# Replacing a six-step gelu with one ScalarE activation, and a sigmoid silu with a tanh form

## The chip, the cores and the metric

The kernel runs on one core of one Trainium2 chip. The metric is the device time of one execution in microseconds (us); where several runs are quoted, it is their median. The profile is one execution taken by the hardware profiler, a little shorter than the device time of the same run (283.6 against 286.2 us before).

Names used below: PE is TensorE (matmul), PEld its weight loads, DVE is VectorE, ACT is ScalarE, POOL is GpSimd, SP issues most DMAs.

## The reference, cut to what matters

Everything is bf16, with S = 2048 rows and D = 512 columns. One branch is local attention (32 heads, 8 shifted keys), the other a two-stage network with gelu; the second gates the first through a silu.

```python
def reference(x, wqkv, wo, w1, w2, w3, w4):
    xn = layernorm(x)
    s  = local_attention(xn @ wqkv) @ wo              # 8 shifted keys per position, softmax
    h  = gelu_tanh(layernorm(xn) @ w1)                # 4 chunks x 4 column blocks = 16 gelus of 128x512
    x1 = xn + shift_columns(h) @ w2
    h2 = gelu_tanh(layernorm(x1) @ w3) @ w4           # F = 1376: 4 chunks x 11 blocks = 44 gelus
    return x + s * silu(x1 + h2)
```

`gelu_tanh` is `jax.nn.gelu(approximate=True)`.

## The kernel before

The 2048 rows are four chunks of 512. A first stage runs, software-pipelined over the chunks: norms (VectorE), transposes, q/k/v and w1 matmuls, attention logits by products on VectorE (`pw`) reduced by TensorE, softmax, w2. Then comes a handover: the third norm needs statistics of all chunks, and its result goes to DRAM and comes back transposed (`x1n_dram`, `x1nT`). After it come a first w3 block, and a main loop that interleaves attention output, `wo`, the next chunk's w3 and w4.

The gelu took three ScalarE and three VectorE instructions (a sigmoid form of the tanh approximation):

```python
    def gelu_from_psum(pt, dst, nparts):
        # ... three scratch tiles sq, xb, t from a pool
        nc.scalar.activation(sq[:nparts], pt[:nparts], AF.Square, scale=SQK)
        nc.scalar.activation(xb[:nparts], pt[:nparts], AF.Copy)
        nc.vector.tensor_scalar(out=sq[:nparts], in0=sq[:nparts], scalar1=1.0, scalar2=None, op0=ALU.add)
        nc.vector.tensor_tensor(out=t[:nparts], in0=sq[:nparts], in1=xb[:nparts], op=ALU.mult)
        nc.scalar.activation(sq[:nparts], t[:nparts], AF.Sigmoid, scale=GELU_C)
        nc.vector.tensor_tensor(out=dst, in0=xb[:nparts], in1=sq[:nparts], op=ALU.mult)
```

Other parts that the argument touches:

```python
            # stage2(c): attention logits, 8 per chunk
            nc.vector.tensor_tensor(out=pw, in0=qT, in1=kT[:, :, koff : koff + CH], op=ALU.mult)
            # ... 16 small matmuls of pw with a head selector, into lg

    # handover: third norm of all 16 row tiles at once, then chunk by chunk
    def stage3b():
        nc.scalar.activation(rstd3, mv3[:, :, 1], AF.Sqrt, bias=eps_t[:], scale=1.0)
        # ... reciprocal, -mean*rstd
    def stage3c(c):
        # ... xn3 = x1 * rstd3 + nmr3
        nc.sync.dma_start(out=x1n_dram[...], in_=xn3)
        nc.sync.dma_start_transpose(out=x1nT, in_=x1n_dram[...])

    def emit_x2(i):                    # attention output of row tile i
        # ... et_ps: transposed softmax; att_sb: its copy
        for w in range(W):             # 8 products on VectorE
            nc.vector.tensor_tensor(out=prod[:, w, :], in0=vs[:, w, :], in1=att_sb[...], op=ALU.mult)
        # ... o_ps: TensorE sums the 8 with an identity matmul; o_sb, ot_ps, oTt

    def emit_final(i, gch, jj):
        # ... pt_s = oTt @ wo
        nc.vector.tensor_tensor(out=sg, in0=pt_s, in1=gch[:, jj, :], op=ALU.mult)
        # ... ot = x + sg, to DRAM

    def emit_w4(c, h3T, gch):
        # ... pt_t = x1 + h3 @ w4
        nc.scalar.activation(sig, pt_t, AF.Sigmoid)
        nc.vector.tensor_tensor(out=gch[:, jj, :], in0=pt_t, in1=sig, op=ALU.mult)
```

The softmax here doesn't subtract the row's maximum and nothing guards it: scores larger than these inputs give would overflow.

## Time and profile before

| | before |
|---|---|
| time, median of 3 runs | 285.42 us (284.32 to 286.18) |
| span of the profiled run | 283.6 us |
| busy PE / DVE / ACT | 236.5 / 230.4 / 180.6 us |
| 60 gelus: ScalarE steps | 597, 601, 635 ns each |
| 60 gelus: VectorE steps | 291, 422, 422 ns each |

From the page of the kernel before: busy time with its share of the span and the number of instructions, then busy tenths in 40 equal slices (each slice is 7.1 us), and the TensorE clock that was granted, in tenths.

```profile
PE 236.5 (83%) x1652; PEld 109.7 (39%) x1680; DVE 230.4 (81%) x586; ACT 180.6 (64%) x318; POOL 7.2 (3%) x26
...
PE   0349978998699999936978899999998999898991
...
DVE  4998998969948986999989958774598992899544
ACT  1105796797569689750469957995178862788620
...
PEclk9999996999999999995899999999999999999997
```

Two engines are above 80% and no slice has TensorE and VectorE idle together, so no single busy share names the limit. The two dips of PE and PEclk in the middle (slices 18 to 20) are the handover.

The chain of work that ended last, shared out by engine, before:

```profile
PE 41%; DVE 30%; ACT 13%; issue 7%; DMA 5%; SPq 2%; ACTq 0%; DVEq 0%
```

So 43% of the chain runs through VectorE and ScalarE.

The same kernel cut into its stages. Columns: window and its length, then busy us of PE, PEld, DVE, ACT, POOL with counts, granted clock, DMA share, GB/s. The rows are: up to the end of the last w1 block; handover; first w3 block; first to last w4 matmul; tail.

```profile
20.00:109.50 89.50, 82.17 (x735) 39.64 (x748) 76.76 (x155) 67.52 (x112) 5.05 (x14) 0.96 0.14 41
109.50:141.00 31.50, 23.64 (x236) 10.29 (x234) 30.96 (x80) 16.18 (x26) 0.00 (x0) 0.84 0.69 189
141.00:158.50 17.50, 13.20 (x75) 5.68 (x74) 15.46 (x51) 14.57 (x27) 0.00 (x0) 1.00 0.85 256
158.50:274.10 115.60, 110.05 (x577) 49.20 (x587) 86.86 (x240) 79.30 (x149) 0.00 (x0) 1.00 0.43 124
274.10:283.60 9.50, 3.65 (x17) 1.46 (x15) 4.51 (x9) 0.60 (x1) 0.00 (x0) 0.82 0.21 69
```

Read each row by itself. In the handover VectorE is full (30.96 of 31.5 us). In the first w3 block VectorE and ScalarE are both near full (15.46 and 14.57 of 17.5) while TensorE needs 13.2. In the long main loop TensorE is at 95%.

What TensorE waited for in the first w3 block of before (total us, times, longest):

```profile
PE w_ps L445 <- ACT g_xb L164: 2.6, 3, 1.3
PE o_ps L411 <- DVE prod L403: 1.4, 1, 1.4
```

Both engines hold it: `g_xb` is a gelu step on ScalarE, `prod` an attention product on VectorE.

The six gelu steps of before, as groups (busy us, mean ns of one, idle time before them and what ended it):

```profile
L167 ACT ACTIVATE g_sq<-g_t 128x512 bf16<-128x512 bf16 (+1 forms) x60 | 37.1, 635 | 3.7 <-DVE g_t L166 3.2
L164 ACT ACTIVATE g_xb<-w_ps 128x512 bf16<-128x512 f32 (+1 forms) x60 | 36.1, 601 | 0.0
L163 ACT ACTIVATE g_sq<-w_ps 128x512 bf16<-128x512 f32 (+1 forms) x60 | 35.8, 597 | 8.0 <-PE w_ps L445 4.4 <-DVE g_t L166 1.4 <-PE w_ps L258 1.0
L166 DVE TENSOR_TENSOR g_t<-g_sq,g_xb 128x512 bf16<-128x512 bf16 (+1 forms) x60 | 25.3, 422 | 4.0 <-ACT g_xb L164 3.9
L168 DVE TENSOR_TENSOR h3T<-g_xb,g_sq 128x512 bf16<-128x512 bf16 (+1 forms) x44 | 18.5, 422 | 2.7 <-ACT g_sq L167 2.1
L165 DVE TENSOR_SCALAR g_sq<-g_sq 128x512 bf16<-128x512 bf16 (+1 forms) x60 | 17.4, 291 | 8.4 <-ACT g_sq L163 7.4
```

(The sixth step writes `h3T` in 44 cases and `hTp` in the 16 of the first stage.)

### The profile page before, as it was taken

To read this page: it belongs to the slowest core of one execution; us is meant where nothing else is said; L and a number is where in the kernel's file an instruction comes from. 1 tells how busy PE (TensorE), PEld (TensorE's weight loads), DVE (VectorE), ACT (ScalarE), POOL (GpSimd) and SP (SyncE) were. 2 spreads that over 40 slices of the span, in tenths; PEclk is the share of its full clock that TensorE was granted. 3 is DMA by queue.
4 is the path that set the end of the run, shared out by engine and by line. 5 is a ranking of instruction groups with operands and counts; after the bars stand their busy time and mean duration, and the time that the engine had idled before them with its cause. 6 is when DMAs were issued, how large, how long until landed. Compare 5 with 4: busy or idle time off the path is not lost.

```text
span 283.6 us, 4696 instructions
## 1 busy us (share of the span) xinstructions
PE 236.5 (83%) x1652; PEld 109.7 (39%) x1680; DVE 230.4 (81%) x586; ACT 180.6 (64%) x318; POOL 7.2 (3%) x26
## 2 busy tenths in 40 slices
PE   0349978998699999936978899999998999898991
PEld 0234444445344444412433344443444444443440
DVE  4998998969948986999989958774598992899544
ACT  1105796797569689750469957995178862788620
POOL 3000100010020001000000000000000000000000
PEclk9999996999999999995899999999999999999997
DMA  7996020020002005853989888514066664111102
GB/s 222 386 376 156 2 74 2 0 77 0 2 0 77 2 0 178 241 157 116 232 238 275 233 247 265 178 38 113 0 177 195 183 192 147 38 37 37 39 0 92
DMA packets 40311, 35.65 MB, mean 126 GB/s; under 512 B 11250, under 2 KB 38752, under 8 KB 40288
## 3 DMA queue, kind: packets, MB, share of 16 engines
q1 hardware_dynamic: 39680, 33.24, 39.5%
q0 software_dynamic: 608, 2.11, 2.2%
q8 instruction: 13, 0.21, 0.3%
q14 instruction: 10, 0.08, 0.1%
HBM read 26.94 MB, written 6.31 MB: 117 GB/s over the span
## 4 chain that ended last, share of the span: by engine, by line
PE 41%; DVE 30%; ACT 13%; issue 7%; DMA 5%; SPq 2%; ACTq 0%; DVEq 0%
PE w_ps L458 12%; PE qk_ps L229 10%; DVE prod L403 6%; DVE pw L269 5%; PE v_ps L246 5%; PE o_ps L411 4%; PE w_ps L445 4%; ACT g_sq L163 4%; DVE g_t L166 3%; ACT g_sq L167 3%; ACT g_xb L164 3%; DMA vs<-v_dram 2%; DVE stats_176 L313 2%; DVE g_sq L165 2%; DVE stats_170 L178 2%
## 5 line engine op out<-in xcount | busy, mean ns | idle before, releaser
L403 DVE TENSOR_TENSOR prod<-vs,att_sb 128x512 bf16<-128x512 bf16 x128 | 49.3, 420 | 2.5 <-DMA vs<-v_dram 2.0
L411 PE MATMUL o_ps<-prod,ident 128*128 128x512 bf16 x128 | 41.2, 402 | 10.9 <-DVE prod L403 10.2
L445 PE MATMUL w_ps<-x1nT,w_sb 128*128 128x512 bf16 (+1 forms) x171 | 46.9, 378 | 2.9 <-ACT g_xb L164 2.6
L458 PE MATMUL w_ps<-w_sb,h3T 128*128 128x512 bf16 (+1 forms) x172 | 41.8, 379 | 0.4
L269 DVE TENSOR_TENSOR pw<-qT,kT 128x2048 bf16<-128x2048 bf16 x32 | 38.5, 1224 | 3.3 <-PE lg L274 1.7
L163 ACT ACTIVATE g_sq<-w_ps 128x512 bf16<-128x512 f32 (+1 forms) x60 | 35.8, 597 | 8.0 <-PE w_ps L445 4.4
L167 ACT ACTIVATE g_sq<-g_t 128x512 bf16<-128x512 bf16 (+1 forms) x60 | 37.1, 635 | 3.7 <-DVE g_t L166 3.2
L164 ACT ACTIVATE g_xb<-w_ps 128x512 bf16<-128x512 f32 (+1 forms) x60 | 36.1, 601 | 0.0
L229 PE MATMUL qk_ps<-xnT,wqkv_sb 128*128 128x512 bf16 x122 | 31.8, 405 | 1.7 <-issue 0.7
L166 DVE TENSOR_TENSOR g_t<-g_sq,g_xb 128x512 bf16<-128x512 bf16 (+1 forms) x60 | 25.3, 422 | 4.0 <-ACT g_xb L164 3.9
L445 PEld LDWEIGHTS <-w_sb 128*128 128x128 bf16 (+1 forms) x176 | 16.9, 99 | 23.4 <-issue 7.4
L465 DVE TENSOR_TENSOR gch<-w_ps,sig 128x512 bf16<-128x512 f32 x16 | 11.0, 690 | 18.3 <-ACT sig L464 18.2
L458 PEld LDWEIGHTS <-h3T 128*128 128x128 bf16 (+1 forms) x176 | 16.6, 98 | 22.1 <-DVE h3T L168 3.7
L165 DVE TENSOR_SCALAR g_sq<-g_sq 128x512 bf16<-128x512 bf16 (+1 forms) x60 | 17.4, 291 | 8.4 <-ACT g_sq L163 7.4
L464 ACT ACTIVATE sig<-w_ps 128x512 bf16<-128x512 f32 x16 | 9.4, 597 | 22.4 <-PE w_ps L462 22.0
L168 DVE TENSOR_TENSOR h3T<-g_xb,g_sq 128x512 bf16<-128x512 bf16 (+1 forms) x44 | 18.5, 422 | 2.7 <-ACT g_sq L167 2.1
L411 PEld LDWEIGHTS <-ident 128*128 128x128 bf16 x128 | 12.8, 101 | 20.5 <-issue 7.6
L229 PEld LDWEIGHTS <-wqkv_sb 128*128 128x128 bf16 x128 | 12.6, 103 | 17.8 <-issue 3.3
L416 ACT ACTIVATE o_sb<-o_ps 128x512 bf16<-128x512 f32 x16 | 9.6, 598 | 15.3 <-PE o_ps L411 15.3
L237 ACT ACTIVATE qT<-qk_ps 128x512 bf16<-128x512 f32 x16 | 9.3, 596 | 13.4 <-PE qk_ps L229 13.4
L195 PE MATMUL rrep_ps<-diag,ones_bf 128*128 128x128 bf16 x16 | 2.9, 247 | 17.9 <-DVE diag L194 17.9
L307 PE MATMUL w_ps<-w_sb,hTp 128*128 128x512 bf16 x59 | 17.1, 381 | 0.6 <-issue 0.5
(89 smaller groups left out, 314.0 us busy)
## 6 DMA issues: line engine op xcount, KB each, us to landing
vs<-v_dram SPq DMA_DIRECT2D x128, 128.0 KB, 2.9
x_all<-in_A_x_dram SPq DMA_DIRECT2D x4, 512.0 KB, 5.4
v_dram<-vct POOLq DMA_DIRECT2D x4, 512.0 KB, 3.3
xtf<-in_A_x_dram SPq DMA_DIRECT2D x16, 128.0 KB, 2.6
out_dram<-ot SPq DMA_DIRECT2D x16, 128.0 KB, 2.0
wqkv_sb<-in_A_wqkv_dram SPq DMA_DIRECT2D x1, 1536.0 KB, 10.6
w_sb<-in_B_w_dram SPq DMA_DIRECT2D x1, 1376.0 KB, 13.6
w_sb<-in_B_w_dram SPq DMA_DIRECT2D x1, 1280.0 KB, 15.9
```

Source lines behind the costliest of these rows:

```text
L163: nc.scalar.activation(sq[:nparts], pt[:nparts], AF.Square, scale=SQK)
L164: nc.scalar.activation(xb[:nparts], pt[:nparts], AF.Copy)
L165: nc.vector.tensor_scalar(out=sq[:nparts], in0=sq[:nparts], scalar1=1.0, scalar2=None, op0=ALU.add)
L166: nc.vector.tensor_tensor(out=t[:nparts], in0=sq[:nparts], in1=xb[:nparts], op=ALU.mult)
L167: nc.scalar.activation(sq[:nparts], t[:nparts], AF.Sigmoid, scale=GELU_C)
L168: nc.vector.tensor_tensor(out=dst, in0=xb[:nparts], in1=sq[:nparts], op=ALU.mult)
L229: nc.tensor.matmul(pt, lhsT=wqkv_sb[:, dt, nt * P : (nt + 1) * P], rhs=xnT[:, dt, :], start=(dt == 0), stop=(dt == ND - 1),)
L269: nc.vector.tensor_tensor(out=pw, in0=qT, in1=kT[:, :, koff : koff + CH], op=ALU.mult)
L403: nc.vector.tensor_tensor(out=prod[:, w, :].rearrange("p (dh h) -> p dh h", dh=DH, h=H), in0=src.rearrange("p (dh h) -> p dh h", dh=DH, h= ...
L411: nc.tensor.matmul(o_ps, lhsT=ident[:], rhs=prod[:, w, :], start=(w == 0), stop=(w == W - 1),)
L445: nc.tensor.matmul(pt[:fs, :], lhsT=w3_sb[:, dt, ft * P : ft * P + fs], rhs=x1nT[:, dt, :], start=(dt == 0), stop=(dt == ND - 1),)
L458: nc.tensor.matmul(pt_t, lhsT=h3T[:fs, ft, jj * P : (jj + 1) * P], rhs=w4_sb[:fs, ft, :], start=(ft == 0), stop=False,)
```

## The change

The intent: take the elementwise gelu work off ScalarE and VectorE by using the hardware's own tanh-gelu, reading PSUM and writing the result in one instruction. The final silu is written with tanh, `silu(x) = 0.5 * x * (1 + tanh(x/2))`, so that it uses a function from the gelu's table set, and the factor 0.5 is folded into `wo` once, by a GpSimd multiply.

```diff
+    nc.gpsimd.tensor_scalar(
+        out=wo_sb, in0=wo_sb, scalar1=0.5, scalar2=None, op0=ALU.mult
+    )
...
     def gelu_from_psum(pt, dst, nparts):
-        (three scratch tiles)
-        nc.scalar.activation(sq[:nparts], pt[:nparts], AF.Square, scale=SQK)
-        nc.scalar.activation(xb[:nparts], pt[:nparts], AF.Copy)
-        nc.vector.tensor_scalar(out=sq[:nparts], in0=sq[:nparts], scalar1=1.0, ..., op0=ALU.add)
-        nc.vector.tensor_tensor(out=t[:nparts], in0=sq[:nparts], in1=xb[:nparts], op=ALU.mult)
-        nc.scalar.activation(sq[:nparts], t[:nparts], AF.Sigmoid, scale=GELU_C)
-        nc.vector.tensor_tensor(out=dst, in0=xb[:nparts], in1=sq[:nparts], op=ALU.mult)
+        nc.scalar.activation(dst, pt[:nparts], AF.Gelu_apprx_tanh)
...
-            nc.scalar.activation(sig, pt_t, AF.Sigmoid)
-            nc.vector.tensor_tensor(out=gch[:, jj, :], in0=pt_t, in1=sig, op=ALU.mult)
+            nc.scalar.activation(sig, pt_t, AF.Tanh, scale=0.5)
+            nc.vector.scalar_tensor_tensor(
+                out=gch[:, jj, :], in0=sig, scalar=1.0, in1=pt_t, op0=ALU.add, op1=ALU.mult
+            )
```

(The two scratch pools also go; cut here.)

More of the change, by code (lines that the diff above doesn't have):

```diff
@@ L44 @@
     PADK = (W - 1) * DIL
-    GELU_C = 1.5957691216057308
-    GELU_K = 0.044715
-    SQK = GELU_K ** 0.5
     CH = 512
@@ L73 @@
     wearly = tc.alloc_tile_pool(name="wearly", side="right", bufs=1)
-    gp1 = tc.alloc_tile_pool(name="gp1", side="right", bufs=3)
     ps_mm = ctx.enter_context(tc.tile_pool(name="ps_mm", bufs=4, space=bass.MemoryType.PSUM))
@@ L153 @@
     nmr3 = small.tile([P, NT], F32, name="nmr3")
-    gp_holder = {}
     def gelu_from_psum(pt, dst, nparts):
-        n = dst.shape[-1]
-        gp = gp_holder["pool"]
-        sq = gp.tile([P, n], BF16, name="g_sq", tag="g_sq")
-        xb = gp.tile([P, n], BF16, name="g_xb", tag="g_xb")
-        t = gp.tile([P, n], BF16, name="g_t", tag="g_t")
-        nc.scalar.activation(sq[:nparts], pt[:nparts], AF.Square, scale=SQK)
-        nc.scalar.activation(xb[:nparts], pt[:nparts], AF.Copy)
-        nc.vector.tensor_scalar(out=sq[:nparts], in0=sq[:nparts], scalar1=1.0, scalar2=None, op0=ALU.add)
-        nc.vector.tensor_tensor(out=t[:nparts], in0=sq[:nparts], in1=xb[:nparts], op=ALU.mult)
-        nc.scalar.activation(sq[:nparts], t[:nparts], AF.Sigmoid, scale=GELU_C)
-        nc.vector.tensor_tensor(out=dst, in0=xb[:nparts], in1=sq[:nparts], op=ALU.mult)
+        nc.scalar.activation(dst, pt[:nparts], AF.Gelu_apprx_tanh)
     xnT_holder = {}
@@ L314, in stage3a @@
             nc.vector.bn_aggr(out=mv3[:, i, :], in_=stats3[:, i, :])
-    gp_holder["pool"] = gp1
     for k in range(NCH + 2):
@@ L323 @@
             stage3a(k - 2)
-    gp1.release()
     wearly.release()
@@ L339 @@
     h3pool = tc.alloc_tile_pool(name="h3pool", side="right", bufs=2)
-    gp2 = tc.alloc_tile_pool(name="gp2", side="right", bufs=2)
-    gp_holder["pool"] = gp2
     sp = tc.alloc_tile_pool(name="sp", side="right", bufs=2)
@@ L499 @@
     sp.release()
-    gp2.release()
     h3pool.release()
```

## The prediction

> **What bounds it now.** Busy table of the profile (span 283.6 us): TensorE 83%, VectorE 81%, ScalarE 64%. The average hides stages.
> - Attention/gelu-1 stage (21 to 122 us): the chain of waits is mostly TensorE, with gelu steps and VectorE `pw` between. The w1 matmuls end at 36.5, 60.2, 86.8, 109.5 (timeline).
> - Handover (122 to 141): VectorE is packed (statistics, softmax sums, `prod`, `xn3`); then a DRAM write of 3.0 us and two transposes. TensorE waits 3.9 and 2.3 us; its granted clock falls to 0.5.
> - First w3 block (141 to 158.5): 17.5 us for about 12 us of TensorE work at 0.217 us per 512-column matmul. ScalarE and VectorE are packed; the waits are on `g_xb` and `prod`.
> - Main loop (158.5 to 274.3): TensorE nearly dense, marked waits under 5 us. Then a 9.3 us tail.
>
> **What the change does.** 60 gelus: 16 in the first stage, 44 later.
> - ScalarE: Square 597, Copy 601, Sigmoid 635 ns become one activation from PSUM, about 0.6 us: the Trainium skill, "ScalarE: Activation LUTs", section "What happens when an exp ACTIVATE runs", says that the cost per element doesn't depend on the function, and the trace agrees (597, 601, 635). Back to back (0.49 us each) ScalarE loses about 65 us: 181 to about 113.
> - VectorE: 291+422+422 ns leave per gelu, about 57 us packed: 230 to about 172.
> - Tanh costs what Sigmoid did, the fused add-multiply what the product did. Table loads: 13 become 12 in the built instruction order; gelu and tanh share a table. The trace and the page's section "What ACT_TABLE_LOAD costs" agree on 1283 ns each.
> - Halving wo is one GpSimd instruction, a few us by estimate from its 0.52 us memset of a quarter of the columns. It delays only the first write of v, unread before about 105 us.
> - TensorE's work is unchanged.
>
> **How much is on the path.** About 120 us of engine work goes, but TensorE's 230 us stay.
> 1. First stage. Chunk 0 to 1: `pw` no longer queues behind gelu pieces, 4 us won. Chunk 1 to 2: nothing (in the new VectorE order both `xnT` copies follow eight `pw`, so TensorE waits 3 to 4 us). Chunk 2 to 3: 1 us at most. Last w1 ends near 105.
> 2. Handover: VectorE still packed, about 1 us won; DMA and transposes keep their 9.6 us. w3 starts near 136.
> 3. First w3 block becomes TensorE-bound: 12 instead of 17.5 us, 5 to 6 won.
> 4. Main loop: about 1 us won; new short stalls where `o_ps` follows `et`, `att_sb` and the first `prod` directly.
> 5. Tail: unchanged.
>
> Sum: about 11.5 us. Predicted 274 us (4% faster), 267 to 280 eight times in ten. Chances: faster 0.90, same 0.09, slower 0.01.
>
> **What would show it.** Step 1: last w1 end at 104 to 107, a wait of `qk_ps` on `xnT` before chunk 2. Step 2: VectorE over 90% busy just before the first `x1n` write, at about 126. Step 3: w3 block of 11 to 13 us with no wait on ScalarE. Step 4: 115 us, within 3, from first to last w4 matmul. Gelu near 600 ns; ScalarE under 120 us busy; VectorE near 172.
>
> **What would make it wrong.** Gelu slower than other functions; a lower granted clock after the handover or with a denser TensorE; the new DMA order (six more `vs` loads before the `x1n` write wait for the first `prod` tile) delaying w3; on the good side, removed pools moving addresses so that `vs` loads start before 105, or the main loop losing more of its 8 us over dense TensorE work.

## The result, and the profile after

| | before | after |
|---|---|---|
| time, median of 4 runs each | 285.37 us | 270.61 us (269.44 to 270.79) |
| ratio, 95% interval | 1 | 0.948 (0.9452 to 0.9509) |
| span of the profiled run | 283.6 us | 269.0 us |

Both outputs match the reference. The change takes 5.2% off; the predicted 274 us was 3.4 us too high, inside its range.

The page of the kernel after (slices of 6.7 us):

```profile
PE 230.8 (86%) x1651; PEld 109.2 (41%) x1680; DVE 178.2 (66%) x406; ACT 121.6 (45%) x197; POOL 12.8 (5%) x27
...
PE   0229968999999999975999999999999999998991
...
DVE  3989999949955953999963237583265842666143
ACT  1102746874575776562267233642336422363310
...
PEclk9999999999999999996599999999999999999998
```

ScalarE lost 59 us and VectorE 52; TensorE is denser. 111 us of engine work went, 14.6 us of span went: nearly all of the removed work ran beside TensorE.

The chain that ended last, after:

```profile
PE 63%; DVE 17%; DMA 9%; SPq 4%; issue 4%; ACT 2%; DVEq 0%
```

The chain is now mainly TensorE.

The stages of the kernel after, in the order of the rows of before:

```profile
20.00:105.30 85.30, 80.48 (x734) 39.00 (x745) 67.55 (x115) 54.84 (x86) 10.65 (x15) 1.00 0.17 47
105.30:136.00 30.70, 24.62 (x238) 10.89 (x241) 30.06 (x77) 12.82 (x20) 0.00 (x0) 0.83 0.75 196
136.00:147.40 11.40, 11.12 (x55) 5.11 (x55) 5.00 (x15) 8.01 (x13) 0.00 (x0) 1.00 0.96 259
147.40:259.30 111.90, 107.95 (x591) 50.15 (x602) 56.05 (x138) 42.91 (x73) 0.00 (x0) 1.00 0.49 138
259.30:269.00 9.70, 3.79 (x18) 1.53 (x16) 4.51 (x9) 0.60 (x1) 0.00 (x0) 0.90 0.23 68
```

Subtract row from row: 4.2 us in the first stage, 0.8 in the handover (VectorE still full, 30.06 of 30.7), 6.1 in the first w3 block (TensorE now fills 11.12 of 11.4), 3.7 in the main loop, -0.2 in the tail. The sum is 14.6.

TensorE's waits in the first w3 block of after:

```profile
PE o_ps L396 <- DVE prod L388: 0.2, 1, 0.2
PE w_ps L430 <- DMA x1nT<-x1n_dram: 0.2, 1, 0.2
```

No wait on ScalarE is left.

One caution about the border of this block. The build placed TensorE's instructions in another order after the change: the block of before has 75 recorded TensorE instructions (13.20 us busy), that of after 55 (11.12 us). Among those that moved are the small `et_ps` transposes of the attention output, 19 recorded in the block before and 2 after; the others now run in the main loop. So a part of the 6.1 us has only crossed the border. The w3 block and the main loop together, 9.8 us, do not depend on where it lies.

The groups of after that answer to the six steps, with the new fused silu product and the halving (line numbers are those of the changed kernel):

```profile
L157 ACT ACTIVATE h3T<-w_ps 128x512 bf16<-128x512 f32 (+1 forms) x44 | 26.1, 597 | 8.8 <-PE w_ps L430 8.6
L450 DVE SCALAR_TENSOR_TENSOR gch<-sig,w_ps 128x512 bf16<-128x512 bf16 x16 | 11.0, 687 | 38.1 <-ACT sig L449 38.1
L157 ACT ACTIVATE hTp<-w_ps 128x512 bf16<-128x512 f32 x16 | 8.5, 600 | 0.0
...
L109 POOL TENSOR_SCALAR wo_sb<-wo_sb 128x2048 bf16<-128x2048 bf16 x1 | 5.4, 5373 | 0.0
```

The gelu costs 597 to 600 ns, what the Square or the Copy alone did, and the fused silu product 687, what the plain one did (690). The Trainium skill, "ScalarE: Activation LUTs", section "Step-by-step: what each stage is for", says that throughput is one element per cycle and lane whatever the function. The trace agrees that the function does not matter: at this one tile size Gelu, Tanh, Square and Copy from PSUM all take 597 to 601 ns. No run here varies the size. (The prediction named the section just above it, which is empty but for a diagram; the statement stands in this one.)

One surprise stands in the trace between 28 and 40 us. The timeline of after (start us, length us, engine, line, instruction, and in brackets the idle time before it with its releaser):

```profile
31.29 5.37 POOL L109 TENSOR_SCALAR wo_sb<-wo_sb 128x2048 bf16<-128x2048 bf16 x1
31.37 5.78 DVE L258 TENSOR_TENSOR pw<-qT,kT 128x2048 bf16<-128x2048 bf16 x2
...
37.28 0.30 ACT L169 ACTIVATE rstd_170<-mv_169,eps_t 128x4 f32<-128x4 f32 x1 [3.68 <-DVE mv_169 L168]
37.48 0.58 ACT L239 ACTIVATE vct<-v_ps 128x512 bf16<-128x512 f32 x1
...
38.11 1.02 PE L247 MATMUL w_ps<-xn2T,w_sb 128*128 128x512 bf16 x4 [1.91 <-ACT vct L239]
```

Read it as a chain. Two `pw` products, which elsewhere take about 2.3 us together, took 5.78 beside the GpSimd halving (4.64 and 1.21 one by one). A small statistics instruction queued behind them, ScalarE waited 3.68 us for it, the eviction of `v` queued behind that, and TensorE waited 1.91 us for a free PSUM buffer in the middle of its w1 block. This is not on the list of things that the prediction counted.

### The profile page after: what moved, and what is told of

Same layout as the page of the kernel before. It is cut to its first block, busy times and chain, and to the rows that moved or that the text cites. A ratio compares the mean times of both kernels' runs of the same rounds, so it can differ in the third digit from the quotient of the medians.

```text
span 269.0 us, 4318 instructions
## 1 busy us (share of the span) xinstructions
PE 230.8 (86%) x1651; PEld 109.2 (41%) x1680; DVE 178.2 (66%) x406; ACT 121.6 (45%) x197; POOL 12.8 (5%) x27
## 4 chain that ended last, share of the span: by engine, by line
PE 63%; DVE 17%; DMA 9%; SPq 4%; issue 4%; ACT 2%; DVEq 0%
PE w_ps L443 14%; PE w_ps L430 12%; PE qk_ps L218 10%; PE o_ps L396 7%; DVE pw L258 5%; DMA wqkv_sb<-in_A_wqkv_dram 5%; PE w_ps L247 4%; PE v_ps L235 4%; DVE prod L388 4%; PE wo_ps L413 3%; PE lg L263 3%; DMA vs<-v_dram 2%; DVE stats_174 L302 2%; SPq L355 2%; PE w_ps L296 2%
## 5 line engine op out<-in xcount | busy, mean ns | idle before, releaser
L258 DVE TENSOR_TENSOR pw<-qT,kT 128x2048 bf16<-128x2048 bf16 x32 | 40.5, 1328 | 17.2 <-PE lg L263 12.7
L388 DVE TENSOR_TENSOR prod<-vs,att_sb 128x512 bf16<-128x512 bf16 x128 | 46.0, 418 | 3.1 <-DMA vs<-v_dram 2.4
L430 PE MATMUL w_ps<-x1nT,w_sb 128*128 128x512 bf16 (+1 forms) x172 | 41.2, 379 | 0.3 <-DMA x1nT<-x1n_dram 0.2
L450 DVE SCALAR_TENSOR_TENSOR gch<-sig,w_ps 128x512 bf16<-128x512 bf16 x16 | 11.0, 687 | 38.1 <-ACT sig L449 38.1
L157 ACT ACTIVATE h3T<-w_ps 128x512 bf16<-128x512 f32 (+1 forms) x44 | 26.1, 597 | 8.8 <-PE w_ps L430 8.6
L443 PEld LDWEIGHTS <-h3T 128*128 128x128 bf16 (+1 forms) x176 | 17.2, 98 | 20.8
L184 PE MATMUL rrep_ps<-diag,ones_bf 128*128 128x128 bf16 x16 | 2.8, 242 | 17.6 <-DVE diag L183 17.3
L413 PE MATMUL wo_ps<-wo_sb,oTt 128*128 128x512 bf16 x60 | 17.6, 378 | 0.1
L418 DVE TENSOR_TENSOR sg<-wo_ps,gch 128x512 bf16<-128x512 f32 x16 | 10.8, 687 | 10.2 <-PE wo_ps L413 10.2
L247 PE MATMUL w_ps<-xn2T,w_sb 128*128 128x512 bf16 x62 | 14.4, 379 | 2.0 <-ACT vct L239 1.9
L301 ACT ACTIVATE x_tm<-w_ps 128x512 bf16<-128x512 f32 x16 | 9.5, 596 | 14.5 <-PE w_ps L300 14.5
L226 ACT ACTIVATE qT<-qk_ps 128x512 bf16<-128x512 f32 x16 | 9.4, 598 | 11.5 <-PE qk_ps L218 9.8
L235 PE MATMUL v_ps<-wv_perm,xnT 128*128 128x512 bf16 x63 | 14.4, 379 | 0.1
```

The lines of the kernel that those rows point to most:

```text
L157: nc.scalar.activation(dst, pt[:nparts], AF.Gelu_apprx_tanh)
L235: nc.tensor.matmul(pt, lhsT=xnT[:, dt, jj * P : (jj + 1) * P], rhs=wv_perm[:, dt, :], start=(dt == 0), stop=(dt == ND - 1),)
L247: nc.tensor.matmul(pt, lhsT=w1_sb[:, dt, g * P : (g + 1) * P], rhs=xn2T[:, dt, :], start=(dt == 0), stop=(dt == ND - 1),)
L388: nc.vector.tensor_tensor(out=prod[:, w, :].rearrange("p (dh h) -> p dh h", dh=DH, h=H), in0=src.rearrange("p (dh h) -> p dh h", dh=DH, h= ...
L413: nc.tensor.matmul(pt_s, lhsT=oTt[:, dt, :], rhs=wo_sb[:, dt, :], start=(dt == 0), stop=(dt == ND - 1),)
L430: nc.tensor.matmul(pt[:fs, :], lhsT=w3_sb[:, dt, ft * P : ft * P + fs], rhs=x1nT[:, dt, :], start=(dt == 0), stop=(dt == ND - 1),)
```

## The experiments

**Theories.** A: the gain is the gelu alone; what came off VectorE and ScalarE counts where those engines were full, and the tanh silu and the saved table load are worth nothing; the GpSimd halving costs about 2 us by blocking VectorE. Rival B: the tanh silu and fewer table loads carry a part of the gain. Rival C: the 5.78 us are an accident of that run. Within A there are two more rivals: that VectorE's time counts, or ScalarE's.

So that the stages can be compared, the next table gives for each profiled run the stretch between fixed TensorE instructions (starts of the first and last w1, first w3, first w4 and last w4 matmul; all in us). The start of the first w1 itself lies between 31.8 and 33.7 us in these runs and is no part of the comparison: the same changed kernel has 33.7 us in its first profiled run and 33.0 in its control.

| run | first to last w1 | to first w3 | to first w4 | to last w4 | to the end |
|---|---|---|---|---|---|
| before | 76.1 | 31.9 | 17.6 | 115.1 | 9.9 |
| after | 71.3 | 31.0 | 11.4 | 111.6 | 10.0 |
| half in the gate product | 69.3 | 31.4 | 11.3 | 111.6 | 9.9 |
| sigmoid silu | 69.3 | 30.9 | 11.1 | 111.7 | 9.8 |
| native silu | 69.3 | 31.1 | 11.2 | 112.2 | 8.6 |
| fused gelu, first stage only | 69.3 | 30.8 | 17.8 | 114.9 | 9.9 |
| fused gelu, w3 only | 75.1 | 32.0 | 13.1 | 111.6 | 9.9 |
| VectorE work given back | 74.3 | 32.1 | 12.9 | 117.0 | 9.9 |
| ScalarE work given back | 70.4 | 30.8 | 16.2 | 109.7 | 9.9 |
| early third norm | 69.3 | 20.1 | 17.5 | 111.5 | 9.8 |

The first four experiments ran on one chip in the same rounds; before was 284.92 us there (median of 11 runs).

### Control: the changed kernel again

No edit.

> Control: the changed kernel as it is, on the same chip as the next three. Every theory: 270.5 us within 1, ratio 0.948 within 0.004.

Measured: 269.6 us (268.3 to 270.95), ratio 0.9465 (0.9427 to 0.9503). The result repeats, and so does the stall: in this profile the two `pw` take 5.59 us beside a halving of 5.38, and ScalarE is again idle for 3.68 us.

### The half moved into the gate product

```diff
-    nc.gpsimd.tensor_scalar(out=wo_sb, in0=wo_sb, scalar1=0.5, scalar2=None, op0=ALU.mult)
...
-        nc.vector.tensor_tensor(out=sg, in0=pt_s, in1=gch[:, jj, :], op=ALU.mult)
+        nc.vector.scalar_tensor_tensor(
+            out=sg, in0=pt_s, scalar=0.5, in1=gch[:, jj, :], op0=ALU.mult, op1=ALU.mult)
```

The order of TensorE's instructions is the same as in the changed kernel.

> The changed kernel, but wo is not halved on GpSimd; the half is a factor in the VectorE instruction that makes sg. TensorE's order is the same. My theory: in the changed kernel's trace two pw products that lie under the 5.4 us GpSimd multiply take 5.8 us instead of 2.3, ScalarE then waits 3.7 us and the w1 matmuls 1.9 us; without the multiply the first w1 block ends 2 to 3 us earlier and the whole is 2 to 3 us faster (267.5 to 268.5), pw mean near 1220 ns. Rival: the multiply and the stall are absorbed later (VectorE has idle time before each later pw); within 0.5 us of the control.

Measured: 267.77 us (266.62 to 268.94), ratio 0.9397 (0.936 to 0.9433): 1.8 us under the control by the medians. The stage table puts 2.0 us of it between the first and the last w1, where the halving sits. The same stretch of the timeline, without the halving:

```profile
30.78 2.34 DVE L254 TENSOR_TENSOR pw<-qT,kT 128x2048 bf16<-128x2048 bf16 x2
...
33.07 3.62 PE L243 MATMUL w_ps<-xn2T,w_sb 128*128 128x512 bf16 x16
33.24 0.30 ACT L165 ACTIVATE rstd<-mv,eps_t 128x4 f32<-128x4 f32 x1 [0.24 <-DVE mv L164]
33.45 0.58 ACT L235 ACTIVATE vct<-v_ps 128x512 bf16<-128x512 f32 x1
```

The pair of products is back at 2.34 us, ScalarE waits 0.24 instead of 3.68 us, and the 16 w1 matmuls run in one piece. The fused product with the half costs what the plain one does. So the halving, one instruction of 5.37 us on an otherwise idle engine, cost the kernel about 2 us; rival C falls, as both profiles with the halving have one `pw` of over 4.4 us, and in the other plain traces, with no GpSimd multiply, none is longer than 1.27.

### The sigmoid silu back

```diff
-            nc.scalar.activation(sig, pt_t, AF.Tanh, scale=0.5)
-            nc.vector.scalar_tensor_tensor(out=gch[:, jj, :], in0=sig, scalar=1.0, in1=pt_t, ...)
+            nc.scalar.activation(sig, pt_t, AF.Sigmoid)
+            nc.vector.tensor_tensor(out=gch[:, jj, :], in0=pt_t, in1=sig, op=ALU.mult)
```

The halving is out as well, since a sigmoid silu needs no half. The built kernel has 19 table loads instead of 12.

> Like e1_half_in_sg, but the final silu is through Sigmoid again, as before the change; TensorE's order is the same, table loads go from 12 to 19. Theory A: ScalarE is idle half of the time in the main loop and the loads fall into waits for TensorE; within 0.7 us of e1_half_in_sg, so the tanh form is worth next to nothing. Theory B: each of the 7 extra loads of 1.28 us delays an eviction that TensorE waits for; 4 to 9 us slower than e1_half_in_sg.

Measured: 267.27 us (266.43 to 267.91), ratio 0.9383 (0.9347 to 0.9418), not to be told from the run above. ScalarE is busier by 8.2 us (129.8 against 121.6) and the time does not show it. The Trainium skill, "ScalarE: Activation LUTs", section "Rules for kernel authors", says to budget about 2.7 us for every switch of the table set, which as an estimate would be 19 us for seven; here seven more loads of 1283 ns cost nothing that could be measured, because they took the place of idle time: ScalarE stood idle for 26.8 us before the 16 silu activations instead of 32.0, and the four loads that stand there take 5.1. Rival B falls: the tanh rewrite brings nothing, and its halving costs 2 us.

### The native silu

```diff
-            (sig tile, Tanh activation, fused product)
+            nc.scalar.activation(gch[:, jj, :], pt_t, AF.Silu)
```

Again without the halving; also 19 table loads.

> Like e1_half_in_sg, but the final silu is one ScalarE activation into gch; no product on VectorE, no half anywhere; 19 table loads. Theory A (loads are hidden): 0 to 1 us faster than e2_sigmoid_back, from the tail alone (0.7 us product left out after the last w4 matmul). Theory B: as slow as theory B of e2_sigmoid_back, 4 to 9 us over e1_half_in_sg.

Measured: 266.85 us (266.23 to 267.93), ratio 0.9368 (0.9334 to 0.9402). VectorE is down to 163.6 us. The tail is 1.3 us shorter (8.6 against 9.9), since the last product is gone from the final chain; the main loop is 0.6 longer. The net of 0.9 us under the half-in-the-gate version lies within the intervals.

### The fused gelu in the first stage only

The next four ran on one chip in the same rounds; before was 284.98 us (median of 7 runs). The four are read against the half-in-the-gate version (ratio 0.9397, a gain of 17.2 us in its own rounds, on another chip, with before at 284.92), since none has the halving.

```diff
     def gelu_from_psum(pt, dst, nparts):
+        if stage == 1:
+            nc.scalar.activation(dst, pt[:nparts], AF.Gelu_apprx_tanh)
+            return
         (the six steps of before)
```

The silu is the sigmoid one of before.

> The kernel before, with the one-instruction gelu in the first stage (16 gelus) only; the second stage and the silu are as before. From the traces: the last w1 block ends at 105 instead of 109.5 and the handover gives about 1 more, so about 5 us faster than before (279 to 281), w3 block still 17 us. No GpSimd multiply here, so the first stage may win 2 us more (277 to 279). Rival (the gain is all in the second stage): under 2 us faster than before.

Measured: 277.38 us (277.03 to 278.08), ratio 0.9722 (0.9677 to 0.9767): 7.6 us won. In the stage table it has the first stage of the half-in-the-gate version (69.3) and the later stages of before (17.8 and 114.9). Its main wait in the w3 block is the one of before:

```profile
PE w_ps L451 <- ACT g_xb L168: 3.5, 4, 1.2
```

### The fused gelu in the w3 stage only

The same edit with `stage == 2`, the tanh silu and the half in the gate product.

> The kernel before, with the one-instruction gelu in the second stage (44 gelus) only, silu through tanh with the half in sg, no GpSimd multiply. From the traces: w3 block 11.5 instead of 17.5 us and the stretch from first to last w4 matmul 112 instead of 115.6: about 9 to 10 us faster than before (275 to 277). If the stages are independent, its gain and that of e4_fused_stage1_only add up to the gain of e1_half_in_sg within 1 us; if the same slack serves both, they add up to over 3 us more or less.

Measured: 276.85 us (275.82 to 277.86), ratio 0.97 (0.965 to 0.975): 8.1 us won. The first stage is close to before (75.1 against 76.1; the 1.0 us is taken up again below, under the clock), the w3 block 13.1 and the main loop 111.6. The two parts add up to 15.7 us against 17.2 for both. That is nearly additive; the missing 1.5 us fell between the two expected outcomes, and the intervals (about 1.4 us to either side of each) do not settle it. The 13.1 us instead of 11.3 in the w3 block is the place in the second stage where the stage table shows less than the half-in-the-gate version gives: TensorE there waited 1.4 us once for `prod`.

### VectorE's share given back

Three VectorE instructions of the old shapes per gelu, on scratch tiles that nobody reads (their pools are cut here). The output stays right. This edit and the next are shown against the half-in-the-gate version.

```diff
         nc.scalar.activation(dst, pt[:nparts], AF.Gelu_apprx_tanh)
+        nc.vector.tensor_scalar(out=sq[:nparts], in0=dst, scalar1=1.0, scalar2=None, op0=ALU.add)
+        nc.vector.tensor_tensor(out=t[:nparts], in0=sq[:nparts], in1=dst, op=ALU.mult)
+        nc.vector.tensor_tensor(out=xb[:nparts], in0=dst, in1=t[:nparts], op=ALU.mult)
```

> e1_half_in_sg with the three VectorE instructions of the old gelu given back for each gelu, on scratch tiles that nobody reads (VectorE load as before, 230 us; ScalarE stays at about 120; the chain of a gelu stays one step). Theory 'VectorE time': gives back 5 us or more in the first stage and the w3 block, 273 to 277. Theory 'length of the chain between two engines': stays within 2 us of e1_half_in_sg.

Measured: 280.27 us (280.02 to 280.83), ratio 0.9823 (0.9779 to 0.9867): 12.5 of the 17.2 us are lost again, more than expected, although nothing reads these results. VectorE is at 226.6 us, ScalarE at 119.9. The loss sits in the first stage (69.3 to 74.3) and in the main loop (111.6 to 117.0), and only 1.6 us in the w3 block. In one stretch of the first stage, 59 to 84 us, TensorE's granted clock was 0.93 in this profile (1.00 without the added work), so a part of the 5.0 us there may be the clock.

### ScalarE's share given back

```diff
+        nc.scalar.activation(sq[:nparts], pt[:nparts], AF.Square)
+        nc.scalar.activation(xb[:nparts], pt[:nparts], AF.Copy)
         nc.scalar.activation(dst, pt[:nparts], AF.Gelu_apprx_tanh)
```

> e1_half_in_sg with two more ScalarE activations from the same PSUM tile for each gelu, into scratch that nobody reads (ScalarE as before, about 180 us; VectorE stays at about 172). Theory 'ScalarE time': the w3 block, where it was packed, goes back to 15 us or more and the main loop loses too, 271 to 276. Theory 'VectorE time only': within 2 us of e1_half_in_sg.

Measured: 270.98 us (270.62 to 272.17), ratio 0.9502 (0.9445 to 0.9558): 3.2 us are lost, at the low end of what was expected if ScalarE's time counted. ScalarE is at 175.0 us, VectorE at 174.7. In the stage table the loss is in the w3 block (11.3 to 16.2), where the old kernel waited for `g_xb`, and the main loop, which was expected to lose too, is 1.9 us shorter. But the 4.9 us of the block are not all loss. The `et_ps` transposes in this block, first without and then with the added ScalarE work:

```profile
L373 PE MATMUL et_ps<-ident,E_c 32*128 32x32 bf16 x2 | 0.2, 178 | 0.0
...
L387 PE MATMUL et_ps<-ident,E_c 32*128 32x32 bf16 x40 | 1.8, 172 | 1.4 <-DVE att_sb L394 1.4
```

The new order has moved 38 of them, 1.6 us of TensorE work, from the main loop into the block, which is about what the loop became shorter by. Block and loop together are free of this: 122.9 us in the half-in-the-gate version, 125.9 with ScalarE's work back, 129.9 with VectorE's, 132.7 before. So of the 9.8 us of these two stages VectorE's work takes back 7.0 and ScalarE's 3.0. Both count, VectorE's more.

These two runs carry a reservation: the scheduler of the build places TensorE's instructions otherwise when instructions are added, so they measure engine time plus what the new order does. The same holds for before against after, whose orders differ as well; how much of the gain the order itself is worth was not tested. The sum of the two, 15.7 of 17.2 us, is as the theory wants it, but it would not notice two errors that cancel.

### GpSimd kept busy

The half-in-the-gate kernel with 20 GpSimd multiplies of 128x2048 on a scratch tile. Nothing makes them wait, so in the trace they run early: all start between 3.8 and 125.1 us.

```diff
+    scr = wlate.tile([P, ND, D], BF16, name="scr")
+    nc.gpsimd.memset(scr[:], 1.0)
+    # two for each chunk in the first stage, three for each chunk in the main loop: 20
+    nc.gpsimd.tensor_scalar(out=scr, in0=scr, scalar1=0.5, scalar2=None, op0=ALU.mult)
```

> A measurement, not a candidate: e1_half_in_sg with 20 GpSimd multiplies of the size of the halving of wo, on a scratch tile, from the start on. Theory 'shared SBUF port': VectorE instructions with two SBUF inputs (pw, xn2T) and those in a fast mode (norm application xn_tm) get longer, some by up to the 5.4 us of a multiply, while those that read PSUM (xnT and rrep copies) and the statistics keep their 0.67 us. Theory 'everything in VectorE slows': all kinds get longer by a similar share. Theory 'the 5.8 us pair was a chance': pw keeps 1220 ns on average.

Measured, one run of unknown state: 350.83 us beside 284.55 for before (median of 7). VectorE's groups in that run:

```profile
L261 DVE TENSOR_TENSOR pw<-qT,kT 128x2048 bf16<-128x2048 bf16 x32 | 47.5, 1542 | 15.6 <-PE lg L266 10.8 <-ACT kT L229 4.8
...
L196 DVE TENSOR_SCALAR xn_tm<-x_all,rstd,nmr 128x512 bf16<-128x512 bf16 x16 | 42.7, 2686 | 0.0
L186 DVE TENSOR_SCALAR diag<-ident,rstd 128x128 bf16<-128x128 bf16 x16 | 27.5, 2385 | 0.0
...
L170 DVE BATCH_NORM_STATS2 stats<-x_all 128x6 f32<-128x512 bf16 x16 | 10.4, 668 | 3.2 <-DMA x_all<-in_A_x_dram 3.2
...
L231 DVE TENSOR_TENSOR xn2T<-xnT,rrep 128x2048 bf16<-128x2048 bf16 x4 | 4.8, 1206 | 0.0
...
L189 DVE CAST rrep<-rrep_ps 128x512 bf16<-128x512 f32 x4 | 2.7, 684 | 0.5 <-PE rrep_ps L187 0.4
```

Without the multiplies the same groups have means of 1220, 404, 245, 668, 1210 and 679 ns. So the two groups with a single source tile and scalars (`xn_tm`, `diag`) became 7 to 10 times as long on average, the two-source `pw` 26% longer, and the statistics and the cast from PSUM did not change. The longest single ones last 5.4 us (`diag`) and 6.3 (`xn_tm`), about one GpSimd multiply (5.37 us in the median, 5.53 on average): such an instruction seems to wait for the end of the multiply that is running.

The Trainium skill, "Advanced Engine Details and Errata", section "Mode Summary", notes that VectorE's second SBUF port is shared with GpSimd and that GpSimd instructions and two-port VectorE instructions block each other; "GPSIMD Engine Reference", section "1. Specifications", adds instructions with two SBUF inputs. Both agree with this run. The averages hide it for two inputs, but the single instructions show it: the six `pw` that ran beside multiplies took 4.65 and 1.21 us in turn, as the pair in the changed kernel did (4.64 and 1.21), while the others took 1.21 to 1.25. The one `xn2T` that ran beside a multiply took its usual 1.21 us, but there the multiply took 6.87 us instead of 5.37, so that time it seems that GpSimd was the one that waited. The run also shows the size, and that the wait is charged to VectorE as busy time.

### Early third norm

The best version that the experiments pointed to: the handover is what the change left alone. The half-in-the-gate kernel with the third norm, the DRAM write and the transpose of chunks 0 and 1 moved into the first stage, and the first w3 block interleaved with the first four attention tiles.

```diff
     for k in range(NCH + 2):
         ...
         if 2 <= k <= NCH + 1:
             stage3a(k - 2)
+            if k - 2 < 2:
+                stage3b(k - 2, k - 1)    # Sqrt of this chunk alone
+                stage3c(k - 2)           # norm, DRAM write, transposed read
...
-    for t_i in range(TPC):
-        emit_x2(t_i)
-    for ft in range(NF):
-        emit_w3(0, h3T, ft)
+    # the four emit_x2 and the eleven emit_w3 in turn
```

> An attempt to beat both: e1_half_in_sg, with the third norm, the DRAM write and the transpose of chunks 0 and 1 moved into the first stage (two more Sqrt table loads on ScalarE), and the first w3 block interleaved with the first four attention tiles. Theory: the handover is a chain (all 16 statistics, norm, write, transpose), not a lack of engine time; with w3 matmuls ready, TensorE fills it and the first w4 matmul comes 6 to 10 us earlier: 258 to 262 us. Rival: VectorE (prod, statistics, softmax sums) is what fills the handover; under 3 us gained.

Measured: 263.46 us (261.51 to 264.6), ratio 0.9246 (0.9191 to 0.9302). It beats both kernels, but by less than expected. From the last w1 to the first w4 it takes 37.6 us instead of 42.7, so 5.1 us were won; the rest of the stages are unchanged, and the main loop did not become shorter. One wait of 2.8 us of `o_ps`, which the profile puts down to the Sqrt of the last chunks, is left in the handover; whether it could be removed was not tried. The 5.1 us lie between the two outcomes (6 to 10, under 3), and the edit changes two things at once, the early norms and the interleaving, so it does not decide between them.

### Early third norm with the native silu, and its control

Run together, with before at 284.18 us (median of 11).

```diff
-            (sig tile, Tanh activation, fused product; half in the gate product)
+            nc.scalar.activation(gch[:, jj, :], pt_t, AF.Silu)
```

> The best version so far with the final silu as one Silu activation and no product after it (7 more table loads, 16 products of 687 ns fewer on VectorE). If VectorE and ScalarE are both off the path of the late loop, as the run with the native Silu in the plain schedule said (0.9 us faster, inside its interval): within 1 us of the same schedule with the tanh silu run beside it, so 262 to 264 us. If VectorE still holds the denser TensorE back: 259 to 262. If table loads begin to hurt where the loop is denser: 265 or more.

> The same kernel as the early-norm run, as its control on this chip: 262 to 265 us, ratio to before 0.919 to 0.930.

Measured: 262.44 us (260.8 to 264.44), ratio 0.9237 (0.9191 to 0.9283) with the native silu; 262.18 us (261.27 to 265.7, one of the six runs slow), ratio 0.9223 (0.9185 to 0.926) for the control. The two are the same: another 10 us off VectorE (174.8 to 164.6) and seven more table loads are worth nothing here. The best version stands at about 0.923 of before.

## Why the prediction was right

The direction, the main mechanism and, within its range, the size were right; 270.6 us measured, 274.0 predicted, range 267 to 280. Some of the closeness is luck: the halving cost 2 us that were not foreseen, and the run without it, at 267.8 us, lies near the lower end of the range. Point by point:

1. **Costs of single instructions: right.** Gelu 597 to 600 ns (predicted about 600), ScalarE 121.6 us (predicted under 120, so just outside, and "about 113" in the text, although 181 less 65 is 116; the 60 gelus did not all run back to back, and their busy time is 34.6 us, 0.58 each instead of 0.49), VectorE 178.2 (predicted near 172). About 4 of VectorE's 6 us too many are the halving: without it VectorE has 174.5. Twelve table loads of 1283 ns each, as the Trainium skill, "ScalarE: Activation LUTs", section "What ACT_TABLE_LOAD costs", has it.
2. **First stage: right sum, wrong parts.** Predicted: last w1 near 105; measured 105.3. But two errors cancel. The text said of the halving that "it delays only the first write of v"; it delayed VectorE and cost 2 us, which the half-in-the-gate run shows. The same run reaches 102.7 (0.6 us of that because its first w1 started earlier). And the prediction expected that from chunk 1 to 2 nothing would be won, because `qk_ps` would wait 3 to 4 us for `xnT`. That wait did not appear: in the trace the transposes that feed the first `xnT` copy start at 67.46 us, behind the w2 matmuls; the copy starts at 68.51, TensorE goes on with other transposes and eight small matmuls, and the dense q/k matmuls start at 69.22, 0.05 us after the copy ends. The period from the end of one w1 block to the next fell from 26.6 to 24.1 us, and before had one wait of 1.7 us for `diag` from VectorE in that stretch, after 0.2. An instruction order tells what an engine does next, not when: the copies stand behind the products in VectorE's order, but the transposes stand as late in TensorE's.
   From chunk 0 to 1, 3.7 us were won (predicted 4), but not all by the gelu. The granted clock in that stretch was 0.86 before and 1.00 after. The run with the fused gelu in the w3 stage only tells the two apart: it has the old gelu and the old TensorE order in the first stage, a clock of 1.00, and needs 22.7 us for the stretch, where before needs 23.7 and after 20.0. So about 1.0 us goes with the clock of that one profile of before, and about 2.7 with the gelu. The Trainium skill, "TensorE: Matmul & The Clock Gate", section "What's actually happening", describes a clock that falls after idle windows; no run here shows what made it fall in this stretch.
3. **Handover: right.** 0.8 us won (predicted 1), VectorE full to the first `x1n` write (16.96 of the 17 us from 109 to 126), that write at 126.3 us (predicted 126), w3 at 136.0 (predicted 136).
4. **First w3 block: right**, with the caution above about its border. 11.4 us (predicted 12, from 17.5), no wait on ScalarE. With ScalarE's work given back 4.9 of the 6.3 us return, but 1.6 of these are transposes moved in from the main loop; with VectorE's, 1.6 return. Both engines held it, as the waits of before said.
5. **Main loop: mis-sized, the term that failed.** The prediction put "about 1 us won" here; 3.7 us were, by the windows, and the measured 111.9 us is just outside the predicted 115 within 3. With the w3 block, whose border moved, it is 9.8 us instead of the 6 to 7 predicted for the two. TensorE was at 95% of the loop, so its marked waits (under 5 us) were taken as nearly all that could be had, and most of these as still there. TensorE's waits in the main loop, before and then after (total us, times, longest):

```profile
PE o_ps L411 <- DVE prod L403: 2.3, 4, 1.0
PE et_ps L392 <- DVE att_sb L399: 1.4, 3, 0.6
...
PE et_ps L377 <- DVE att_sb L384: 1.9, 5, 0.4
PE o_ps L396 <- DVE prod L388: 0.8, 1, 0.8
```

   With the third of before (`ot_ps` on ScalarE's `o_sb`, 1.0 us) they fell by only 2.0 us, from 4.7 to 2.7. TensorE's busy time in the loop fell as well, from 110.05 to 107.95 us, although more instructions were recorded there (591 against 577). So the 95% busy share hid time that could be won; busy is not the same as dense. The VectorE work alone, given back, makes this loop 5.4 us longer, and the two waits on VectorE grow to 4.0 (`prod`) and 3.4 (`att_sb`); the fused gelu in the first stage alone leaves the loop at 114.9; and ScalarE's work given back does not lengthen it, apart from the transposes that left it. The loop's reserve lay on VectorE. The prediction did name this case among those that would make it wrong ("the main loop losing more of its 8 us over dense TensorE work"), but gave it no number. The expected new stalls at `et_ps` are small: five in all, 1.9 us, the longest 0.4; before had three, 1.4 us in all.
6. **Tail: right**, 9.7 us after 9.5.

The sum as predicted was 11.5 us; the sum as measured in the profiles is 14.6. The main loop is 2.7 of the 3.1 us between them; the other stages together account for the remaining 0.4.

The sentence that carried the prediction, that about 120 us of engine work goes but TensorE's work stays, holds: 111 us went and the time fell by about 13% of that.

## What to carry to other kernels

Cost a removal stage by stage, from the engine that is full in that stage, and subtract: here 111 us of removed work were worth 15, and the main loop, where TensorE was already 95% busy, still gave a quarter of it. Compare stages only after checking that the same instructions lie in them: a build may move work across a border. Do not put "free" work on an idle GpSimd while VectorE works between SBUF tiles: one 5.4 us multiply cost 2 us, and folding the factor into an existing two-operand VectorE instruction cost nothing. Before saving table loads, look whether anything waits for ScalarE: here seven more of them made no measurable difference.

## What the Trainium skill lacked or had wrong

- The skill says that GpSimd and VectorE block each other; that the profile counts this wait as VectorE's busy time was found in no page. Here `diag` went from 0.25 us to 2.39 on average and `xn_tm` from 0.40 to 2.69, with the longest at 5.4 and 6.3 us.
- No page has the time of a bf16 GpSimd multiply by a constant: 128x2048 took 5.37 us in the changed kernel, and 5.37 in the median and 5.53 on average in the run with 20 of them.
- "ScalarE: Activation LUTs", section "Table sets: the hidden batching unit", lists `gelu_and_others` as separate from the tanh-approximated gelu and does not say where that one lives. The kernel with gelu and tanh has 12 loads, with gelu and sigmoid or silu 19, so in this build the approximated gelu and tanh share a set, and sigmoid and silu are not in it.
- The same page's section "Rules for kernel authors" budgets about 2.7 us for each switch. That can be ScalarE's own time (the load itself took 1283 ns in every trace here), but the row does not say that a load can fall into idle time of ScalarE and then cost the kernel nothing: seven more loads made no measurable difference (267.27 against 267.77 us).
